# Products of zeros ahead of the first chunk, one weight tile's low part moved from TensorE to VectorE, and a new set of plan numbers, in a kernel that joins linear attention with a gated feed-forward

## The chip, the cores and the metric

The kernel runs on one NeuronCore of a Trainium2 chip. The metric is device time in microseconds (us), as the median of several runs. A profile of one execution goes with it; its time is not one of the runs that make the median. TensorE does the matrix products ("PE" in the rows, "PEld" its weight loads), VectorE is "DVE", ScalarE is "ACT", GpSimd is "POOL", and SyncE ("SP") issues the DMAs.

## The reference

For 4 batches and 8 heads, a state of 48 x 48 decays row by row, takes in the outer product of key and value at each of 768 steps, and is read by the query. The 3072 tokens that come out (384 numbers each) go through an RMS norm and a gated feed-forward with 1536 inner columns.

```python
for t in range(S):
    state = alpha[:, :, t, :, None] * state + np.einsum('bhd,bhe->bhde', k[:, :, t], v[:, :, t])
    y[:, :, t] = np.einsum('bhd,bhde->bhe', q[:, :, t], state)
...
rms = np.sqrt(np.mean(x * x, axis=-1, keepdims=True) + 1e-06)
xn = x / rms * rms_g
g = xn @ w_gate
silu = g * (1.0 / (1.0 + np.exp(-g)))
val = xn @ w_val
return (silu * val @ w_out).astype(np.float32)
```

## The kernel before

**Chunks and groups.** The tokens are cut into 24 chunks of 128 (6 of each batch; chunks 0 to 3 are the first of each batch). Seven groups of 4, 2, 2, 4, 4, 4 and 4 chunks go through the feed-forward one after the other. In group 0 the first five of the twelve inner tiles are done for chunks 0 and 1 and then for chunks 2 and 3, so that the feed-forward can begin when two chunks are there.

**Attention of a chunk.** VectorE runs two scans over the decays (`w`, line 643, with a small reciprocal at 663 between them), multiplies query and key by them (`qp` at 680 in two halves, `kh` at 673). For chunks 0 to 3 everything stays in float32: TensorE turns the keys (line 875), makes the scores (760); VectorE masks them (776); TensorE makes the output `y` (786), the new state (890, in two halves) and the state's part of the output (795); ScalarE squares and sums the output (942), GpSimd takes the root (946, 947), VectorE scales (956, tile `x`), and TensorE turns the result (963, `mm_x`), of which ScalarE takes the high half (971), TensorE subtracts it (977) and ScalarE takes the rest (980). The result is `xT`, the input of the feed-forward. Later chunks work on float16 halves (lines 750, 817, 838, 915).

**Feed-forward.** Each float32 operand is a high and a low float16 half, so that a product takes three passes. For an inner tile f, TensorE multiplies `xT` with the gate and the value weights (line 1131, nine products each); ScalarE makes the silu (1142), VectorE the product with it (1148, called the gate below), ScalarE its high half (491) and VectorE its low half (1161). Line 1201 multiplies with the output weights, VectorE copies out (1212), and SP stores.

**Weights.** A tile of weights (`i0` to `i11` for gate and value, `o0` to `o5` for the output) is loaded as bytes of float64 and made float32 by a ScalarE step (525, the fold) and two VectorE steps (`shift` 530, `join` 533); ScalarE makes the high half (491). The low half is made by VectorE (line 541), but for the tiles named in `LOW_W` by TensorE and ScalarE: two float32 products with a scaled unit matrix (550), from which two float16 products with `minus` (553) take the high half away, and two ScalarE copies (556).

**Order.** Nothing is scheduled by the compiler. `Plan.order` makes one list from a table of costs (`COST`), due times (`DUE`, `GAP`) and shifts (`LATE`, `W_LATE`): at each step the engine that can start first takes, among what can start within 0.12 of that, the operation with the smallest due number. The list is then issued as it stands, and each engine runs its own part strictly in that order. PSUM has three buffers `mm`, three `at` and one `y`.

**Set-up.** Constants are filled by GpSimd and VectorE in the first 6 us. `junk` is a bfloat16 tile of 128 x 384 into which the squares are thrown; its first row serves as `unit`, a row of float32 ones by which TensorE spreads the norm's gains over all partitions (line 614, `mm_rg`).

Of the kernel before, what the change touches and what calls it, by code (L numbers as in the profile page):

```python
# [8 lines left out]
F32 = mybir.dt.float32  # L9
# [41 lines left out]
WIDE = range(10, 24)  # L51
LOW_H = ()
LOW_X = range(4)
LOW_W = ("i0", "i1")

BUFS = dict(
    att=3, w=1, v=3, kh=2, qp=2, k16=2, q16=2, kT=2, v16=4, gd=2, a16=2, ss=2, x32=1, x16=2,
# [1 line left out]
)  # L59

COST = dict(
    scan=1.16, rec=0.13, kh=0.6, qh=0.33, kl=0.6, vl=0.47, ql=0.62, gd=0.12, sd=0.28, sl=0.27, mask=0.59,
    al=0.59, st=0.27, ss=0.12, x=0.46, xl=0.47, shift=0.53, rest=0.88, wl=0.87, ob=0.46,
    dec=0.15, k16=0.62, v16=0.52, q16=0.62, s16=0.26, a16=0.5, sq=0.58, x16=0.53, st0=0.22,
    abs=0.86, odd=0.57, cnt=1.0, wh=0.83, pow=0.8, sc=0.76, sc32=0.9, ys=0.42, ysw=0.38, yv=0.63, yvw=0.57, y32=0.9, add=0.5, take=0.4, u=0.5, po=1.48, xp=0.75, kp=1.3, u32=0.42,
    neg=0.3, wid=0.85, wneg=0.22, wl2=0.37, rgw=0.9, rgt=0.37, x32=0.53, xb=0.37, ys32=0.5, kb=0.45, near=0.34, xneg=0.25,
)
IN_COST = {
    4: (1.95, 0.49, 0.6, 0.63), 3: (1.47, 0.39, 0.47, 0.52), 2: (0.99, 0.28, 0.34, 0.4),
# [4 lines left out]


PACE = [1.0, 1.0, 1.15, 1.18, 1.18, 1.18, 1.18]
GAP = [-5.4, 137.5, 45.8, 79.0, -35.5, -147.4, 300.1]
DUE = [
    -693.9, -491.0, 464.9, -444.6, 227.3, 564.4, 969.3, 214.1, 305.6, 685.2, 893.3, 575.6, 395.1,
    645.7, 528.3, 156.8, 1104.0, 734.3, 817.3, 300.8, 329.7, 361.1, 414.6, 337.4,  # L80
]
LATE = dict(
    a16=97.6, abs=61.6, add=41.2, al=-52.5, cnt=178.7, dec=-135.3, gd=141.7, k16=-182.6, kb=-58.3,
    kh=169.5, kl=74.7, kp=-158.1, ld2=171.2, load=150.3, mask=-114.5, near=72.9, ob=-130.4,
    odd=-190.2, pow=57.4, q16=-118.1, qh=59.8, ql=-30.8, rec=59.8, rest=-78.3, rg=96.3, rgt=-181.3,
    rgw=49.9, s16=7.8, sc=-119.5, sc32=-44.1, scan=250.6, sd=20.3, shift=-35.4, sl=-33.6, sq=106.5,
    st=-123.9, st0=-164.3, take=-51.2, u=-134.6, u32=-60.7, v=169.9, v16=42.6, vl=19.2, wh=190.9,
    wid=-61.7, wl=-196.0, wl2=37.2, wneg=29.8, x=-243.3, x16=-28.4, x32=0.1, xb=-1.8, xl=32.9,
    xneg=81.0, xp=1.9, y32=-23.6, ys=-23.1, ys32=-39.7, ysw=-28.6, yv=-16.5, yvw=-100.7,
)  # L90
LATE_CHECK = 3
W_LATE = [
    -329.2, -491.3, -215.9, -189.0, -124.1, -113.7, -147.5, 9.7, 26.7, -144.3, 45.6, 99.3, 11.9,
    31.8, 264.2, 289.5, 212.6, 338.9,
]
CUTS = [0, 2, 4]
SIDE = [3, 1]


class Plan:  # L100
# [9 lines left out]
    def op(self, engine, cost, fn, deps=(), use=(), due=None, lock=False, kb=0, late=0.0, kind=None, tile=None):  # L110

        o = dict(e=engine, c=cost, fn=fn, d=[d for d in deps if d], u=tuple(use), due=due, lock=lock,
                 kb=kb, late=late, i=len(self.ops), n=[], k=kind, w=tile)
        for d in o["d"]:
            d["n"].append(o)
        for k in o["u"]:
            self.users[k] = self.users.get(k, 0) + 1
        self.ops.append(o)
        return o
# [216 lines left out]
def tile_attn_moe(  # L336
# [12 lines left out]
    nc = tc.nc  # L349
    NC, _, AW = att.shape  # L350
    R = 112
    DM, DFF = w_gate.shape
    P = 128
# [12 lines left out]
    const = ctx.enter_context(tc.tile_pool(name="const", bufs=1))  # L366
# [3 lines left out]
    xp = ctx.enter_context(tc.tile_pool(name="xp", bufs=1))  # L370
# [5 lines left out]
    ps_mm = ctx.enter_context(tc.tile_pool(name="ps_mm", bufs=1, space=PSUM))  # L376
# [18 lines left out]

    plan = Plan()

    def buf(pool, shape, dtype, tag, key):
        name = "_".join(map(str, key)) if isinstance(key, tuple) else key
        return pool.tile(  # L400
            shape, dtype, tag=f"{tag}{plan.slot[tag, key]}", name=f"{tag}_{name}", bufs=1
        )
# [6 lines left out]
    def att_tile(cc):  # L409
        return tile_of(("att", cc), lambda: buf(ain, [P, AW], F32, "att", cc))  # L410
# [4 lines left out]
    def load_v(cc):  # L415
        v = buf(ain, [P, DM], F32, "v", cc)
        tiles["v", cc] = v
        nc.sync.dma_start(v, vtok[src(cc)])
# [5 lines left out]
    rg = const.tile([P, DM], F32, name="rg")  # L424


    seed = const.tile([R, 2, NP, HC + 1], F32, name="seed")
    nc.vector.memset(seed, 0.0)
    nc.vector.memset(seed[:, 0, :, 0:1], S_Q[1] / S_QP)
# [4 lines left out]
    mask = const.tile([P, 1, C], F32, name="mask")  # L434
    near = const.tile([P, 1, HC], F32, name="near")
# [8 lines left out]
    for x, base, step in (  # L444
# [3 lines left out]
            x, x, pattern=[[0, 1], [1, x.shape[-1]]], compare_op=ALU.is_ge, fill=0.0,  # L448
# [9 lines left out]
    for x, value in ((minus, -1.0), (one, 1.0), (same, S_W)):  # L458
        nc.gpsimd.affine_select(
            x, x, pattern=[[1, P]], compare_op=ALU.not_equal, fill=value, base=0,  # L460
# [6 lines left out]
    nc.gpsimd.memset(t_add, T_ADD)  # L467
    mhalf = const.tile([P, 1], F32, name="mhalf")
    nc.gpsimd.memset(mhalf, -0.5)
    junk = const.tile([P, DM], mybir.dt.bfloat16, name="junk")  # L470
    unit = junk.bitcast(F32)[:1, :P]
    nc.gpsimd.memset(unit, 1.0)


    NH = len(GROUPS) * NF + EARLY * (len(CUTS) - 2)
    o_w, o_o = NC, NC + NF
# [11 lines left out]
    dec = const.tile([R, NC, 2, NP], F32, name="dec")  # L488
# [11 lines left out]
    op = plan.op  # L500

    def add(engine, kind, *args, **kw):
        w = kw.get("tile")
        late = LATE.get(kind, 0.0) + (W_LATE[w] if w is not None else 0.0)
        return op(engine, COST[kind], *args, late=late, kind=kind, **kw)
# [3 lines left out]
    def decode(src, dst, name, col):  # L509
# [3 lines left out]
        def load():  # L513
            raw = buf(wst, [P, NW], I64, "raw", name)
            h = 8 * NW // len(src)
            for i, ap_in in enumerate(src):
                k, w = ap_in.shape[1:]
                to = raw.bitcast(U8)[:, i * h : (i + 1) * h].rearrange("p (k b) -> p k b", k=k)
                nc.sync.dma_start(to[:, :, :w], ap_in)
            t["z"], t["t"] = [raw.bitcast(I32).rearrange("p (n two) -> p n two", two=2)[:, :, i] for i in range(2)]  # L520
            t["tf"] = raw.bitcast(F32).rearrange("p (n two) -> p n two", two=2)[:, :, 1]
            t["top"] = raw.bitcast(I8).rearrange("p (n b) -> p n b", b=8)[:, :, 7 - W_FROM]
# [40 lines left out]
        o = add("DVE", "rest", join, [o, f], [raw, wu], lock=True, tile=w)  # L563
        if name in LOW_W:
            ps = [("at", (name, n)) for n in range(2)]
# [37 lines left out]

    states = {}
    state_ops = {}

    def load_rg():
        nc.sync.dma_start(rg[:1], rms_g.unsqueeze(0))
# [638 lines left out]
    def in_steps(g):  # L1247

        if g:
            return [(f, 0, GROUPS[g]) for f in range(NF)]  # L1250
        return [
            (f, c0, c1) for c0, c1 in zip(CUTS, CUTS[1:]) for f in range(EARLY)
        ] + [(f, 0, GROUPS[0]) for f in range(EARLY, NF)]
# [33 lines left out]
    for g, m in enumerate(GROUPS):  # L1287
        now += GAP[g]
        for i in range(m if g else 0):
# [186 lines left out]
```

## Time and profile before

| | |
|---|---|
| median of 3 runs (lowest, highest) | 521.84 us (520.71, 522.1) |
| the profiled execution: its own time, its span from first to last instruction | 521.89 us, 520.2 us |
| busy share of the span: PE, DVE, ACT, POOL | 97%, 74%, 49%, 7% |
| chain that ended last, by engine: PE, DVE, ACT | 86%, 8%, 2% |

Busy time is the time in which an engine had an instruction in work. The chain is followed back from the last instruction: at each step to what released it, or to the instruction before it on its engine. "Idle before" is the time in which the engine had nothing in work ahead of an instruction, with what ended that. A float32 product is two records in the profile. The granted TensorE clock is given as a share of 2.4 GHz.

### The profile page before, as it was taken

The page shows a single profiled execution, that of the slowest core. Times are in us where ns is not written, and L with a number is a line of the kernel's source. Part 1 is how long each engine was busy: PE and PEld are TensorE (multiplying, and loading weights), DVE is VectorE, ACT ScalarE, POOL GpSimd, SP SyncE. Part 2 cuts the span into 40 slices and gives each one's busy share as a digit, 9 for nine tenths or more (in the row PEclk, how much of TensorE's full clock was granted, in tenths as well). Part 3 has the DMA queues.
Part 4 walks back from the last instruction along what each step waited for, and adds up shares of the span by engine and source line. Part 5 has one row for each costly group of instructions (what it writes and reads, how often), then busy time and mean ns, then how long its engine had stood idle before and what let it go on. Part 6 is the DMA issues. An engine that isn't in the chain of part 4 may idle for free.

```text
span 520.2 us, 12190 instructions
## 1 busy us (share of the span) xinstructions
PE 504.3 (97%) x4976; PEld 303.5 (58%) x4976; DVE 385.7 (74%) x731; ACT 254.0 (49%) x671; POOL 37.9 (7%) x86
## 2 busy tenths in 40 slices
PE   4899999999999999999999999999999999999995
PEld 3687854567877886544566544556544456444552
DVE  6879999999999999998799979997454320233303
ACT  2478977634563575644654466656454310233200
POOL 4020000020010011000010001203100000000000
PEclk9999999999999999999999999999999999999999
DMA  8869686635455346462097661208960000000000
GB/s 303 285 217 231 187 244 208 207 101 151 80 114 154 122 70 140 91 147 80 17 252 213 174 217 38 33 15 246 307 208 31 1 15 32 15 1 0 2 32 33
DMA packets 64031, 65.18 MB, mean 125 GB/s; under 512 B 32993, under 2 KB 57570, under 8 KB 63970
## 3 DMA queue, kind: packets, MB, share of 16 engines
q1 hardware_dynamic: 63970, 64.36, 44.2%
q8 instruction: 39, 0.64, 0.5%
q14 instruction: 22, 0.18, 0.1%
HBM read 52.03 MB, written 4.72 MB: 109 GB/s over the span
## 4 chain that ended last, share of the span: by engine, by line
PE 86%; DVE 8%; ACT 2%; issue 1%; DMA 1%; POOL 0%; DVEq 0%; ACTq 0%; POOLq 0%
PE mm L1131 47%; PE mm_po L1201 27%; PE at L750 3%; PE y L838 2%; PE at L915 2%; DVE wu_i L533 1%; PE y L817 1%; DVE h L1148 1%; PE y L786 1%; DVE h L1161 1%; DVE w L643 1%; PE at L875 1%; DVE wg L541 1%; PE at_i L550 1%; PE mm_x L963 1%
## 5 line engine op out<-in xcount | busy, mean ns | idle before, releaser
L1131 PE MATMUL mm<-xT,wg 128*128 128x512 f16 (+1 forms) x1602 | 287.3, 339 | 0.5 <-ACT sl L1142 0.5
L1131 PEld LDWEIGHTS <-wg 128*128 128x128 f16 x1602 | 153.7, 98 | 121.1 <-issue 0.4
L1201 PE MATMUL mm_po<-wo,h 128*128 128x384 f16 x864 | 144.4, 326 | 0.2 <-DVE h L1148 0.2
L1201 PEld LDWEIGHTS <-h 128*128 128x128 f16 x864 | 83.1, 98 | 56.1 <-issue 1.7
L1148 DVE SCALAR_TENSOR_TENSOR h<-mm,sl 128x512 f32<-128x512 f32 (+1 forms) x89 | 51.7, 583 | 48.4 <-PE mm L1131 48.2
L491 ACT ACTIVATE h<-h 128x512 f16<-128x512 f32 (+1 forms) x89 | 48.5, 545 | 75.2 <-DVE h L1148 74.9
L1142 ACT ACTIVATE sl<-mm 128x512 f32<-128x512 f32 (+1 forms) x89 | 45.4, 510 | 50.7 <-PE mm L1131 50.1
L1161 DVE TENSOR_TENSOR h<-h,h 128x512 f16<-128x512 f32 (+1 forms) x89 | 51.5, 584 | 21.3 <-ACT h L491 21.3
L643 DVE TENSOR_TENSOR_SCAN w<-att,seed 112x520 f32<-112x520 f32 x48 | 59.4, 1238 | 2.6 <-DMA att<-att 2.1
L1212 DVE TENSOR_SCALAR ob<-mm_po 128x384 f32<-128x384 f32 x24 | 13.1, 550 | 36.1 <-PE mm_po L1201 36.0
L946 POOL TENSOR_TENSOR ss<-ssq,eps 128x1 f32<-128x1 f32 x24 | 13.0, 542 | 331.6 <-ACT junk L942 331.6
L766 DVE TENSOR_TENSOR at<-at,mask 128x512 f32<-128x512 f32 x40 | 25.9, 690 | 1.8 <-PE at L750 1.5
L865 ACT CAST a<-at 128x512 f16<-128x512 f32 x40 | 22.6, 583 | 8.1 <-DVE at L766 8.0
L868 DVE TENSOR_TENSOR a<-at,a 128x512 f16<-128x512 f32 x40 | 25.9, 683 | 0.0
L680 DVE TENSOR_TENSOR qp<-att,w 112x256 f32<-112x256 f32 x48 | 18.4, 420 | 3.5 <-PE y L795 3.4
L947 POOL TENSOR_TENSOR ss<-ss,mhalf 128x1 f32<-128x1 f32 x24 | 18.8, 783 | 1.9
L491 ACT ACTIVATE k<-kh 112x512 f16<-112x512 f32 x20 | 12.6, 628 | 10.2 <-DVE kh L673 9.4
L491 ACT ACTIVATE q<-qp 112x512 f16<-112x512 f32 x20 | 12.5, 623 | 10.4 <-DVE qp L680 5.6
L750 PEld LDWEIGHTS <-k 48*128 48x128 f16 x480 | 13.4, 94 | 6.3 <-issue 5.1
L666 ACT COPY dec<-w 112x8 f32<-112x8 f32 x24 | 4.9, 203 | 24.9 <-DVE w L643 24.8
L750 PE MATMUL at<-q,k 48*128 48x128 f16 x480 | 16.9, 217 | 0.0
L491 ACT ACTIVATION_READ_ACCUMULATOR h<-h 128x1 f32 x89 | 16.7, 188 | 0.0
(129 smaller groups left out, 449.1 us busy)
## 6 DMA issues: line engine op xcount, KB each, us to landing
att<-att SPq DMA_DIRECT2D x22, 773.0 KB, 4.5
v<-vtok SPq DMA_DIRECT2D x24, 192.0 KB, 3.9
out_dram<-ob SPq DMA_DIRECT2D x24, 192.0 KB, 2.0
raw_c<-w_gate SPq DMA_DIRECT2D x12, 384.0 KB, 4.9
raw_c<-w_val SPq DMA_DIRECT2D x12, 384.0 KB, 5.8
raw_d<-w_out SPq DMA_DIRECT2D x6, 768.0 KB, 4.6
raw_i<-w_gate SPq DMA_DIRECT2D x11, 384.0 KB, 3.9
raw_i<-w_val SPq DMA_DIRECT2D x11, 384.0 KB, 4.5
```

The costliest lines, as they stand in the source:

```text
L491: nc.scalar.activation(dst, src, AF.Copy, scale=scale, accum_out=stat[:rows, col : col + 1])
L643: nc.vector.tensor_tensor_scan(w, x, start.rearrange("r g p c -> r (g p c)"), 0.0, op0=ALU.mult, op1=ALU.add)
L750: nc.tensor.matmul(t["sc"][j][:, p, :], t["k16"][r, x, p, :], t["q16"][r, y, p, :], start=m == 0, stop=m == 2,)
L766: nc.vector.tensor_tensor(t["sc"][j], t["sc"][j], mask.to_broadcast([P, NP, C]), op=ALU.mult)
L865: nc.scalar.copy(a_tile()[:, j, 0], t["sc"][j])
L868: nc.vector.tensor_tensor(a_tile()[:, j, 1], t["sc"][j], a_tile()[:, j, 0], op=ALU.subtract)
L947: nc.gpsimd.tensor_tensor(t["ss"], t["ss"], mhalf, op=ALU.pow)
L1131: nc.tensor.matmul(ps[:, :n], wg[:, f, x, j, kk, :], xT[:, y, kk, cs], start=i == 0, stop=i == 3 * NK - 1,)
L1142: nc.scalar.activation(t["sl"][:, :n], t[0][:, :n], AF.Silu, scale=1.0 / (S_X * S_W))
L1148: nc.vector.scalar_tensor_tensor(t["h"][:, :n], t[1][:, :n], S_H / (S_X * S_W), t["sl"][:, :n], op0=ALU.mult, op1=ALU.mult,)
L1161: nc.vector.tensor_tensor(h16_of(g, f)[:, 1, cs], t["h"][:, :n], h16_of(g, f)[:, 0, cs], op=ALU.subtract)
L1201: nc.tensor.matmul(t[i][:, :DM], h16_of(g, f)[:, x, ts], wo[:, f // 2, y, f % 2, :], start=f == 0 and m == 0, stop=f == NF - 1 and m == 2,)
```

## The change

Fourteen bfloat16 products of 128 x 128 by 128 x 384 (`warm_first`) stand ahead of everything else on TensorE. Their operands are the tile `junk`, which VectorE now fills with zeros at the start (its first row with the float32 ones); GpSimd's fill of that row goes. They write a buffer `mm` that nobody reads. `LOW_W` loses `i1`, so that this tile's low half is made by VectorE's line 541 (now 544). Some costs and all due numbers and shifts of the plan have new values, which changes the order on every engine; the amount of work of every other kind stays. The new file has ten lines more: line 643 is now 653, 875 is 885, 1131 is 1141, and 530, 533, 550 are 533, 536, 553.

```diff
-LOW_W = ("i0", "i1")
+LOW_W = ("i0",)
...
-GAP = [-5.4, 137.5, 45.8, 79.0, -35.5, -147.4, 300.1]
+GAP = [-15.7, 137.0, 36.9, 106.2, -22.7, -134.2, 399.9]
...
+WARM_FIRST = 14
...
+    junk = const.tile([P, DM], mybir.dt.bfloat16, name="junk")
+    unit = junk.bitcast(F32)[:1, :P]
+    nc.vector.memset(junk, 0.0)
+    nc.vector.memset(unit, 1.0)
     seed = const.tile([R, 2, NP, HC + 1], F32, name="seed")
...
-    junk = const.tile([P, DM], mybir.dt.bfloat16, name="junk")
-    unit = junk.bitcast(F32)[:1, :P]
-    nc.gpsimd.memset(unit, 1.0)
...
+    def warm_first():
+        ps = buf(ps_mm, [P, 512], F32, "mm", "warm")
+        for _ in range(WARM_FIRST):
+            nc.tensor.matmul(ps[:, :DM], junk[:, :P], junk, start=True, stop=True)
+
+    op("PE", 4.8, warm_first, [], [("mm", "warm")])
```

TensorE at the program's start, before (`mm_rg` spreads the gains, `kh_0` is the key of chunk 0, `at` and `y` are PSUM tiles):

```order
L614 MATMUL mm_rg_170<-rg_90,junk_135 128x384
L875 MATMUL at_0_4_183<-one_115,kh_0_181 128x112 x4
L760 MATMUL at_0_0_194<-qp_0_177,kh_0_181 64x64 x2
L760 MATMUL at_0_1_195<-qp_0_177,kh_0_181 64x64 x2
...
```

and now:

```order
L613 LDWEIGHTS junk_91
L613 MATMUL mm_warm_150<-junk_91 128x384
...
L613 MATMUL mm_warm_150<-junk_91 128x384
L624 MATMUL mm_rg_188<-rg_90,junk_91 128x384
L885 MATMUL at_0_4_199<-one_118,kh_0_197 128x112 x4
L770 MATMUL at_0_0_208<-qp_0_193,kh_0_197 64x64 x2
L770 MATMUL at_0_1_209<-qp_0_193,kh_0_197 64x64 x2
...
```

Fourteen pairs of load and product now stand ahead of the first useful product; they wait for VectorE's fill of the row of ones, its third instruction.

VectorE between the second chunk's key and the third chunk's scans, before (`wu_i1`, `wu_i0` are weight tiles in work, `a16_1` the masked scores of chunk 1, `x32_0` the scaled output of chunk 0):

```order
L530 TENSOR_SCALAR wu_i1_302<-raw_i1_162 128x768
L680 TENSOR_TENSOR qp_2_307<-att_2_158,w_2_249 112x4x64 x2
L776 TENSOR_TENSOR a16_1_310<-at_1_0_284,near_98 128x256
L776 TENSOR_TENSOR a16_1_310<-at_1_1_285,near_98 128x256
L533 SCALAR_TENSOR_TENSOR wu_i1_302<-raw_i1_162,wu_i1_302 128x768
L956 SCALAR_TENSOR_TENSOR x32_0_318<-y_0_220,ss_0_312,rg_90 128x384
L673 TENSOR_TENSOR kh_2_326<-att_2_158,w_2_249 112x2x4x64
L530 TENSOR_SCALAR wu_i0_334<-raw_i0_174 128x768
L533 SCALAR_TENSOR_TENSOR wu_i0_334<-raw_i0_174,wu_i0_334 128x768
L643 SCALAR_TENSOR_TENSOR w_3_373<-att_3_190,seed_91 112x520
```

and now:

```order
L533 TENSOR_SCALAR wu_i1_300<-raw_i1_178 128x768
L690 TENSOR_TENSOR qp_2_320<-att_2_171,w_2_265 112x4x64
L536 SCALAR_TENSOR_TENSOR wu_i1_300<-raw_i1_178,wu_i1_300 128x768
L786 TENSOR_TENSOR a16_1_327<-at_1_0_302,near_101 128x256
L786 TENSOR_TENSOR a16_1_327<-at_1_1_303,near_101 128x256
L690 TENSOR_TENSOR qp_2_320<-att_2_171,w_2_265 112x4x64
L544 SCALAR_TENSOR_TENSOR wg_146<-wu_i1_300,wg_146 128x768
L966 SCALAR_TENSOR_TENSOR x32_0_339<-y_0_234,ss_0_329,rg_90 128x384
L533 TENSOR_SCALAR wu_i0_342<-raw_i0_190 128x768
L683 TENSOR_TENSOR kh_2_348<-att_2_171,w_2_265 112x2x4x64
L536 SCALAR_TENSOR_TENSOR wu_i0_342<-raw_i0_190,wu_i0_342 128x768
L653 SCALAR_TENSOR_TENSOR w_3_372<-att_3_206,seed_94 112x520
```

The low half of `i1` (line 544) now stands on VectorE ahead of the scaling of chunk 0, and the join of `i1` ahead of the mask of chunk 1.

TensorE right behind the scores of chunk 1, before, with the float32 products of both weight tiles:

```order
L550 MATMUL at_i1_0_320<-wu_i1_302,same_114 128x384
L963 MATMUL mm_x_0_328<-one_115,x32_0_318 128x128 x3
L550 MATMUL at_i1_1_337<-wu_i1_302,same_114 128x384
L786 MATMUL y_1_342<-v_1_166,a16_1_310 64x48 x16
...
L553 MATMUL at_i1_1_337<-wg_145,minus_112 128x384
L795 MATMUL y_1_342<-sd1_379,qp_1_218 64x48 x8
L550 MATMUL at_i0_0_394<-wu_i0_334,same_114 128x384
L550 MATMUL at_i0_1_400<-wu_i0_334,same_114 128x384
```

and now:

```order
L973 MATMUL mm_x_0_344<-one_118,x32_0_339 128x128 x3
L796 MATMUL y_1_350<-v_1_186,a16_1_327 64x48 x16
L987 LDWEIGHTS minus_115
L987 MATMUL mm_x_0_344<-xT_0_370,minus_115 128x384
...
L553 MATMUL at_i0_0_389<-wu_i0_342,same_117 128x384
L805 MATMUL y_1_350<-sd1_394,qp_1_251 64x48 x8
L553 MATMUL at_i0_1_408<-wu_i0_342,same_117 128x384
```

The two products of `i1` are gone, so that behind the scores of chunk 1 TensorE's next instruction is the turn of chunk 0, which waits for VectorE's `x32_0`.

On SP, the load of chunk 2's `att` now stands ahead of chunk 0's `v`, of the second part of chunk 1's `att` and of the weights `i1`.

## Rows read from the trace of the kernel before

**Rows 1.** The page's first part: busy us, share of the span and instructions of each engine.

```profile
PE 504.3 (97%) x4976; PEld 303.5 (58%) x4976; DVE 385.7 (74%) x731; ACT 254.0 (49%) x671; POOL 37.9 (7%) x86
```

**Rows 2.** Busy time by stretch: its us, then PE, PEld, DVE, ACT, POOL busy us (instructions), the granted clock, the DMA engines' share and GB/s.

```profile
0.00:20.00 20.00, 12.19 (x162) 10.14 (x162) 14.07 (x26) 5.73 (x13) 6.10 (x35) 1.00 0.87 313
40.00:60.00 20.00, 18.74 (x328) 15.96 (x327) 19.07 (x38) 17.84 (x51) 1.48 (x4) 1.00 0.85 212
60.00:120.00 60.00, 59.77 (x491) 34.14 (x489) 58.98 (x103) 39.71 (x94) 2.97 (x2) 1.00 0.65 192
120.00:240.00 120.00, 120.00 (x1656) 84.73 (x1655) 116.80 (x246) 64.64 (x199) 6.85 (x14) 1.00 0.48 113
240.00:360.00 120.00, 120.00 (x1240) 65.42 (x1237) 108.87 (x206) 68.83 (x182) 13.51 (x18) 1.00 0.47 128
```

**Rows 3.** TensorE in one piece (timeline: start us, us, what), two pieces of the chain late in the program (start us, us, what), and the only wait of TensorE from 62 us on (us in total, times, longest).

```profile
57.04 37.24 PE L1131 MATMUL mm<-xT,wg 128*128 128x256 f16 x216
```

```profile
373.18 46.62 PE mm L1131 x216
419.80 23.40 PE mm_po L1201 x144
```

```profile
PE mm_po L1201 <- DVE h L1148: 0.2, 1, 0.2
```

**Rows 4.** The chain that ended last, at the start of the program: start us, us, what.

```profile
8.10 2.05 PE at L875 x8
...
11.80 1.96 PE y L786 x30
...
18.19 1.05 PE at L760 x30
```

**Rows 5.** TensorE's timeline from 18 to 38 us: start us, us, line, operation, tiles, shapes, records, and in brackets the idle time before and what ended it.

```profile
21.03 1.62 PE L550 MATMUL at_i<-wu_i,same 128*128 128x384 f32 x2 [1.80 <-DVE wu_i L533]
...
25.14 1.63 PE L786 MATMUL y<-v,a 64*64 64x48 f32 x32
26.70 0.34 PE L977 MATMUL mm_x<-xT,minus 128*128 128x384 f16 x1
26.97 0.66 PE L890 MATMUL at<-v,kT 64*64 64x48 f32 x16
...
28.07 0.67 PE L795 MATMUL y<-sd,qp 48*64 48x48 f32 x16
28.67 1.56 PE L550 MATMUL at_i<-wu_i,same 128*128 128x384 f32 x4
30.06 0.49 PE L553 MATMUL at_i<-wg,minus 128*128 128x384 f16 x2
...
31.07 1.15 PE L875 MATMUL at<-one,kh 112*128 112x112 f32 x8
32.15 0.69 PE L760 MATMUL at<-qp,kh 48*64 48x64 f32 x32
32.77 0.94 PE L963 MATMUL mm_x<-one,x 128*128 128x128 f32 x6
33.54 1.04 PE L875 MATMUL at<-one,kh 112*128 112x112 f32 x8
34.52 1.08 PE L786 MATMUL y<-v,a 64*64 64x48 f32 x30
...
37.64 0.61 PE L1131 MATMUL mm<-xT,wg 128*128 128x256 f16 x4
```

**Rows 6.** What VectorE waited for up to 34 us: us in total, times, longest.

```profile
DVE qp L680 <- PE y L795: 3.4, 2, 2.3
...
DVE a L776 <- PE at L760: 1.2, 2, 0.7
...
DVE x L956 <- POOL ss L947: 0.4, 1, 0.4
DVE wu_i L533 <- ACT raw_i L525: 0.4, 1, 0.4
```

**Rows 7.** VectorE's timeline, with columns as in rows 5.

```profile
12.66 0.69 DVE L673 TENSOR_TENSOR kh<-att,w 112x512 f32<-112x512 f32 x1
...
20.80 0.61 DVE L956 SCALAR_TENSOR_TENSOR x<-y,ss,rg 128x384 f32<-128x384 f32 x1
...
28.79 0.76 DVE L680 TENSOR_TENSOR qp<-att,w 112x256 f32<-112x256 f32 x2 [2.31 <-PE y L795]
```

**Rows 8.** Groups of VectorE instructions of one shape over the whole span: busy us, mean ns of one, idle before.

```profile
L643 DVE TENSOR_TENSOR_SCAN w<-att,seed 112x520 f32<-112x520 f32 x48 | 59.4, 1238 | 2.6 <-DMA att<-att 2.1
...
L541 DVE SCALAR_TENSOR_TENSOR wg<-wu_i,wg 128x768 f16<-128x768 f32 x10 | 9.5, 945 | 0.0
```

**Rows 9.** Two stretches of the tail, with columns as in rows 2.

```profile
514.00:515.00 1.00, 0.61 (x4) 0.16 (x2) 0.36 (x2) 0.00 (x0) 0.00 (x0) 1.00 0.00 0
...
518.00:519.00 1.00, 0.00 (x0) 0.00 (x0) 0.00 (x0) 0.00 (x0) 0.00 (x0) 0.50 0.02 8
```

**Rows 10.** The program's start in the timeline of all engines, with columns as in rows 5.

```profile
0.98 0.49 DVE L428 MEMSET seed<- 112x520 f32 x1 [0.98 <-PEq L1465]
...
3.73 1.24 DVE L643 TENSOR_TENSOR_SCAN w<-att,seed 112x520 f32<-112x520 f32 x1 [2.11 <-DMA att<-att]
...
6.16 1.65 PE L614 MATMUL mm_rg<-rg,junk 1*128 1x384 f32 x2 [6.16 <-POOL junk L472]
```

More of the change, by code (lines that the diff above doesn't have):

```diff
@@ L61 @@
 COST = dict(
-    scan=1.16, rec=0.13, kh=0.6, qh=0.33, kl=0.6, vl=0.47, ql=0.62, gd=0.12, sd=0.28, sl=0.27, mask=0.59,
+    scan=1.16, rec=0.18, kh=0.6, qh=0.33, kl=0.6, vl=0.47, ql=0.62, gd=0.12, sd=0.28, sl=0.27, mask=0.59,
     al=0.59, st=0.27, ss=0.12, x=0.46, xl=0.47, shift=0.53, rest=0.88, wl=0.87, ob=0.46,
-    dec=0.15, k16=0.62, v16=0.52, q16=0.62, s16=0.26, a16=0.5, sq=0.58, x16=0.53, st0=0.22,
-    abs=0.86, odd=0.57, cnt=1.0, wh=0.83, pow=0.8, sc=0.76, sc32=0.9, ys=0.42, ysw=0.38, yv=0.63, yvw=0.57, y32=0.9, add=0.5, take=0.4, u=0.5, po=1.48, xp=0.75, kp=1.3, u32=0.42,
-    neg=0.3, wid=0.85, wneg=0.22, wl2=0.37, rgw=0.9, rgt=0.37, x32=0.53, xb=0.37, ys32=0.5, kb=0.45, near=0.34, xneg=0.25,
+    dec=0.2, k16=0.62, v16=0.52, q16=0.62, s16=0.26, a16=0.5, sq=0.58, x16=0.53, st0=0.28,
+    abs=0.86, odd=0.57, cnt=1.0, wh=0.83, pow=0.8, sc=0.76, sc32=0.8, ys=0.42, ysw=0.38, yv=0.63, yvw=0.57, y32=1.12, add=0.5, take=0.4, u=0.5, po=1.48, xp=0.9, kp=1.15, u32=0.66,
+    neg=0.3, wid=0.85, wneg=0.33, wl2=0.37, rgw=0.7, rgt=0.37, x32=0.53, xb=0.37, ys32=0.66, kb=0.5, near=0.34, xneg=0.28,
 )
@@ L76 @@
 PACE = [1.0, 1.0, 1.15, 1.18, 1.18, 1.18, 1.18]
-GAP = [-5.4, 137.5, 45.8, 79.0, -35.5, -147.4, 300.1]
+GAP = [-15.7, 137.0, 36.9, 106.2, -22.7, -134.2, 399.9]
 DUE = [
-    -693.9, -491.0, 464.9, -444.6, 227.3, 564.4, 969.3, 214.1, 305.6, 685.2, 893.3, 575.6, 395.1,
-    645.7, 528.3, 156.8, 1104.0, 734.3, 817.3, 300.8, 329.7, 361.1, 414.6, 337.4,
+    -719.9, -428.4, 411.3, -551.6, 184.4, 443.0, 1038.8, 186.9, 211.3, 740.5, 1018.7, 654.7, 756.4,
+    831.8, 770.0, 432.6, 1179.9, 1019.1, 1109.0, 512.2, 336.7, 338.7, 475.6, 483.2,
 ]
 LATE = dict(
[L83 to L89, printed above, removed]
+    a16=95.7, abs=95.5, add=-3.0, al=-37.8, cnt=239.3, dec=-143.8, gd=128.7, k16=-225.5, kb=-100.3,
+    kh=211.5, kl=37.3, kp=-148.6, ld2=204.9, load=96.2, mask=-127.2, near=132.3, ob=-144.7,
+    odd=-153.0, pow=73.9, q16=-96.0, qh=38.4, ql=-11.4, rec=52.2, rest=-69.8, rg=8.7, rgt=-201.8,
+    rgw=-6.4, s16=44.3, sc=-125.2, sc32=-36.5, scan=303.9, sd=70.9, shift=-71.0, sl=-52.1, sq=109.6,
+    st=-82.7, st0=-193.5, take=-59.8, u=-107.2, u32=-53.5, v=186.2, v16=124.3, vl=-14.9, wh=160.7,
+    wid=-93.7, wl=-301.4, wl2=15.7, wneg=80.9, x=-230.4, x16=-36.5, x32=-16.4, xb=-7.0, xl=-43.5,
+    xneg=126.0, xp=27.6, y32=-52.5, ys=-23.6, ys32=-78.8, ysw=-43.9, yv=-74.0, yvw=-116.3,
 )
@@ L92 @@
 W_LATE = [
-    -329.2, -491.3, -215.9, -189.0, -124.1, -113.7, -147.5, 9.7, 26.7, -144.3, 45.6, 99.3, 11.9,
-    31.8, 264.2, 289.5, 212.6, 338.9,
+    -285.5, -492.0, -249.7, -250.4, -99.8, -149.6, -106.2, -73.2, 53.8, -132.7, 151.4, 126.2, 126.8,
+    172.8, 286.5, 195.7, 182.1, 333.3,
 ]
+WARM_FIRST = 14
 CUTS = [0, 2, 4]
```

## The prediction

> **What bounds the kernel now.** I read the page's busy shares first: TensorE 97%, VectorE 74% [rows 1]. A share over the whole span hides stages, so the second view is busy time by stretch [rows 2]: in the first 20 us TensorE is busy for 12.19 us and VectorE for 14.07; from 40 to 240 us VectorE has hardly a gap (19.07 of 20, 58.98 of 60, 116.80 of 120), and only behind 240 does it get room (108.87 of 120). TensorE's timeline shows from where it is full: at 57.04 us one piece of 216 feed-forward products begins, and from 62 us on its only wait is 0.2 us [rows 3]. Late in the program, where nothing disturbs it, 216 wide products take 46.62 us (216 ns each) and 144 output products 23.40 us (162.5 ns each) [rows 3]: that is a stream without holes. So behind 57 us the time is TensorE's work, and the time of the end moves by what is earlier at 57 us and by what TensorE no longer has to do, as long as VectorE, which is full up to 240 us, keeps up.
>
> Ahead of 57 us I read the chain and the timeline. From 8.10 to about 27 us the chain is nearly all TensorE [rows 4], and the same instructions take longer there than later: eight records of line 875 take 2.05 us at 8.10 and 1.15 and 1.04 us at 31.07 and 33.54; line 786 takes 1.96 at 11.80, 1.63 at 25.14 and 1.08 at 34.52; two records of line 550 take 1.62 at 21.03, and four take 1.56 at 28.67 [rows 4, 5]. That is a factor near 2, TensorE's two clock levels, 1.2 and 2.4 GHz, with the rise between 25.14 and 26.97. The granted clock in the profile's rows reads 1.00 from the start [rows 2]: it shows no change there, the durations do. Only the fall at the end is recorded (0.50 from 518 us, after the last product in the microsecond from 514) [rows 9]. VectorE pays for the low clock in waits for TensorE: 3.4 us ahead of `qp`, 1.2 us ahead of the masks, and 0.4 + 0.4 for others, 5.4 us in all [rows 6].
>
> **The change, part by part.**
>
> *The zeros.* No row shows such a product. The nearest, 384 columns at the high clock, takes 162.5 ns [rows 3]; at half the clock that is 325. Fourteen take 2.3 to 4.6 us. They can start when VectorE has filled `junk`, `seed` and the row of ones: 0.98 + 0.49 for `seed` [rows 10], and by that row at most 0.49 for `junk`, so near 2.0 us, and they end by 6.6. VectorE's first scan waits for its DMA until 3.73, so the fills cost nothing. Behind them `mm_rg` takes 1.65 us at most [rows 10] and ends by 8.2; line 875 of chunk 0 waits for `kh` until 8.10. Cost 0 to 0.1 us; I take 0.
>
> *The clock.* If it is up when chunk 0 arrives, the pieces of [rows 4] shrink to the later durations of [rows 5]. The waits of VectorE go: the scores of chunk 0 come 0.9 us sooner (line 875 alone), which ends the first mask's wait; `qp` of chunk 2 and the mask of chunk 1 wait no more. Up to `x32_0`, which began at 20.80 [rows 7], that is 1.1 (the first of the two `qp` waits, 3.4 less the 2.31 at 28.79 [rows 6, 7]) + 1.2 = 2.3 us. The moved low half puts 0.9 us back (mean 945 ns [rows 8]). So `x32_0` begins near 19.4 and ends near 20.0 us.
>
> From there I count TensorE's queue in the new order to the first feed-forward product, by the later rows of [rows 5], from 26.70 on: turn 0.94, `y` of chunk 1 1.08, line 977 0.34, line 890 0.66, the two products of `i0` 1.56, line 795 0.67, line 553 0.49, line 890 0.66, then chunk 3 and 2: 1.15, 0.69, 0.94, 1.04, 1.08, 0.66, 0.34, 0.69, 0.67. Sum 13.7, so the first one starts at 33.7 instead of 37.64: 3.9 us earlier. In this sum lies what the change takes from TensorE: two float32 products and two subtractions of `i1`, 1.56 + 0.49 = 2.05 us at the high clock. ScalarE loses two copies; it is not the bound.
>
> *VectorE.* It gains 5.4 us of waits; I leave 0.4 of them, since the waits for GpSimd and ScalarE may stay: 5.0. It gets 0.9 of low half, and by the order one more scan (1.24 [rows 8]) stands ahead of the last copy-out of group 0; all other kinds are as many as before up to there. That leaves 2.9 us by which VectorE is earlier where it is full.
>
> *The loads.* Ahead of chunk 0's `v` now stand 2.0 MB; at the 313 GB/s of the first 20 us [rows 2] they land by 8 us, and line 786, which wants `v`, began at 11.80 [rows 4]. Cost 0.
>
> *The rest of the plan.* Behind 57 us TensorE has 0.2 us of waits to win [rows 3], so a new order can only lose there, or nothing. Bounds: 0 to 1 us of loss; I take 0.
>
> *Sum.* TensorE's count gives 3.9 us, VectorE's 2.9. VectorE bounds where it has no gap, to 240 us, but the feed-forward takes its results with three PSUM buffers between, which lets it lag by part of a step. I take 3.4, the middle: 521.89 - 3.4 = 518.5 for an execution like the profiled one, which lies 0.05 above the median of the runs: 518.4.
>
> **A rule that speaks against it.** Between 11.80 and 19.23 us TensorE works in the chain without a break [rows 4], and the clock stays low; the small float32 products did not lift it, so they may not hold it either. In the new order TensorE has nothing to do from the end of chunk 1's scores (near 16.1: the key of chunk 1, 13.35 before [rows 7], comes 0.5 sooner without the first mask's wait, then 1.15 + 0.67 + 0.66 + 0.69) to `x32_0` at 20.0, a hole of nearly 4 us; in the tail the fall is on record some 3 us after the last product [rows 9]. The Trainium skill (TensorE: Matmul & The Clock Gate, section "HAM oscillation") says that idle gaps between bursts of products send the clock back to half, each burst then starting slow. The tail agrees. By that rule the change's gain would end at the hole; this is the second case below.
>
> **The rivals.**
>
> 1. *The clock falls in the hole.* Then the queue from 20.0 runs at half speed until full-size products lift it, as those from 21.03 on did some 5 us later [rows 5]. In 5.3 us it does work of 2.7: the first feed-forward product comes near 36.3 instead of 33.7, and 1.3 us of the gain remain by TensorE. VectorE keeps about 1 us of its second `qp` wait: 2.9 - 1 = 1.9. Middle 1.6: 520.2 us.
>
> 2. *The change doesn't do what it says: zeros don't lift the clock.* Then the waits stay but for what the order changes (the join of `i1` now lies in the mask's wait): VectorE wins back about 2.4 us of 5.4 and pays 0.9 + 1.24, so 0.3; TensorE's removed products, 3.2 at the low clock (twice 1.62 of line 550 [rows 5]), are eaten by a later `x32_0` and by a clock that rises later. About 521.6 us, no change. Against it: nothing in the trace says what zeros do.
>
> 3. *Slower: the clock rises later than before.* What stands right ahead of the rise in before are full-size float32 products, among them both of `i1` (21.03 and on, [rows 5]), and these go. If the zeros don't hold and TensorE then stays at half speed until 32 us or later, 5 us more at half speed cost 2.5 us at a place where TensorE has no gaps, against 0.3 to 0.9 us gained: 523.5 us. The turning point is a rise near 28 us.
>
> 4. *More than counted:* VectorE follows TensorE's 3.9 and some loss between 40 and 57 us goes too (20 - 18.74 us [rows 2]): 5 us, 516.8.
>
> **How the numbers follow.** The forecast holds 0.57, with its own range of 517.4 to 519.4; rival 1 holds 0.19, rival 2 0.09, rival 3 0.10, rival 4 0.05. A change of less than 0.3% (1.57 us) can't be told from none, so "faster" is below 520.3. The forecast and rival 4 lie there (0.62), with half of rival 1 (0.09): 0.71. "Same" takes the other half and most of rival 2, 0.18; "slower" is rival 3 and a bit of rival 2, 0.11. The range reaches over rivals 1 and 2 and leaves out most of rivals 3 and 4: 516.9 to 521.7.
>
> **What would show it.** Line 885 (old 875) of chunk 0 near 1.15 us for eight records, and the float32 products of lines 796 and 553 at the durations of [rows 5], mean that the clock was up and held; doubled durations behind 20 us mean rival 1, from the start on rival 2. VectorE's waits up to 34 us should fall from 5.4 to under 1 us. The first feed-forward product should start near 34 us, and the full stream near 53.5 instead of 57.04. Behind that, TensorE's waits should stay under 1 us; if VectorE's gate becomes a wait of several us between 60 and 240 us, the extra 2.1 us on VectorE were what decided, and the forecast is too good.

## The result, and the profile after

The changed kernel takes **525.26 us** (median of 13 executions, 520.7 to 531.1) against 521.79 us for the kernel before in the same runs (13, 520.71 to 522.53): ratio **1.0064, 95% interval 1.0039 to 1.0089**. The prediction was 518.4 us with a range of 516.9 to 521.7: the direction is wrong, and the median lies outside. The spread grew too, from 1.8 us to 10.4 us. The profiled execution took 523.55 us (span 521.7), so it is one of the quicker ones; what a longer one looks like is read from a second profile, below.

The views of before have their counterparts here; lines of the program lie 3 to 10 higher (550 is now 553, 875 is 885, 1131 is 1141). First, the page's busy shares, as in [rows 1]:

```profile
PE 508.2 (97%) x4984; PEld 305.8 (59%) x4984; DVE 387.9 (74%) x734; ACT 254.3 (49%) x669; POOL 30.9 (6%) x85
```

Then busy time by stretch, with the columns of [rows 2]:

```profile
0.00:20.00 20.00, 16.75 (x176) 12.09 (x176) 14.83 (x27) 6.13 (x14) 6.30 (x34) 1.00 0.88 310
20.00:40.00 20.00, 18.00 (x259) 14.12 (x260) 16.31 (x30) 11.42 (x30) 2.05 (x5) 1.00 0.72 216
40.00:60.00 20.00, 19.09 (x270) 16.36 (x268) 19.90 (x38) 17.66 (x52) 1.75 (x3) 1.00 0.84 228
60.00:120.00 60.00, 58.27 (x547) 33.80 (x546) 58.27 (x103) 40.50 (x95) 1.81 (x4) 1.00 0.64 187
120.00:240.00 120.00, 120.00 (x1581) 84.86 (x1579) 112.50 (x235) 62.85 (x195) 5.47 (x14) 1.00 0.43 108
```

In the first 20 us TensorE is busy for 4.56 us more than before; 4.66 us of that are the zeros. Behind 20 us TensorE is busy for less in two stretches: 60 to 120 us (58.27, where 59.77 stood) and 20 to 40 us (18.00, where 18.96 stood in this row of before):

```profile
20.00:40.00 20.00, 18.96 (x272) 14.73 (x273) 16.75 (x30) 12.90 (x32) 2.99 (x4) 1.00 0.67 213
```

VectorE has more room from 120 to 240 us (112.50 of 120, 116.80 before), so it didn't become the bound there.

TensorE's timeline, with the columns of [rows 5]:

```profile
1.87 4.66 PE L613 MATMUL mm_warm<-junk 128*128 128x384 bf16 x14 [1.87 <-DVE seed L436]
6.46 1.64 PE L624 MATMUL mm_rg<-rg,junk 1*128 1x384 f32 x2
8.29 2.02 PE L885 MATMUL at<-one,kh 112*128 112x112 f32 x8 [0.19 <-DVE kh L683]
...
22.00 1.65 PE L973 MATMUL mm_x<-one,x 128*128 128x128 f32 x6 [2.62 <-DVE x L966]
23.58 1.95 PE L796 MATMUL y<-v,a 64*64 64x48 f32 x32
...
26.91 1.65 PE L553 MATMUL at_i<-wu_i,same 128*128 128x384 f32 x2
28.49 1.09 PE L805 MATMUL y<-sd,qp 48*64 48x48 f32 x16
29.51 1.65 PE L553 MATMUL at_i<-wu_i,same 128*128 128x384 f32 x2
...
31.52 0.66 PE L900 MATMUL at<-v,kT 64*64 64x48 f32 x16
32.11 1.15 PE L885 MATMUL at<-one,kh 112*128 112x112 f32 x8
...
38.43 4.76 PE L1141 MATMUL mm<-xT,wg 128*128 128x256 f16 x42
```

Fourteen zeros in 4.66 us are 333 ns each: the low clock. Line 885 takes 2.02 us, as before the change; in this execution the zeros did not lift the clock at all. And the durations halve only near 31 us (line 900 at 31.52, line 885 at 32.11), while in before they did so near 26 [rows 5]. The first feed-forward product starts at 38.43 instead of 37.64.

VectorE's waits up to 34 us, as in [rows 6], and the waits of TensorE over the whole span:

```profile
DVE qp L690 <- PE y L805: 3.5, 2, 2.4
...
DVE a L786 <- PE at L770: 1.1, 2, 0.6
...
DVE x L966 <- POOL ss L957: 0.4, 1, 0.4
```

```profile
PE mm_x L973 <- DVE x L966: 3.0, 2, 2.6
...
PE mm_po L1211 <- issue: 1.7, 1, 1.7
```

Of 5.4 us of VectorE's waits 0.4 went. The wait of 1.7 us ahead of line 1211 stands at 103.4 us; the profile names no releaser for it.

**Where the time of this execution went.** Idle time of TensorE by the stretches above and [rows 2]: 0 to 20 us 7.81 before, 3.25 after (the zeros fill it); 20 to 40 us 1.04 and 2.00; 40 to 60 us 1.26 and 0.91; 60 to 120 us 0.23 and 1.73: 2.45 less in all, while it is busy for 3.9 us more, so the span grows by 1.5 us. Without the zeros TensorE's busy time is 503.5 instead of 504.3: two products and two subtractions went, but what stands between 26 and 31 us ran at half speed and gave most of that back. The 1.5 us is about as large as the gap at 103.4 us; the expected gain ahead of it never came.

### The profile page after: what moved, and what is told of

Same layout as the page of the kernel before. It is cut to its first block, busy times and chain, and to the rows that moved or that the text cites. A ratio compares the mean times of both kernels' runs of the same rounds, so it can differ in the third digit from the quotient of the medians.

```text
span 521.7 us, 12197 instructions
## 1 busy us (share of the span) xinstructions
PE 508.2 (97%) x4984; PEld 305.8 (59%) x4984; DVE 387.9 (74%) x734; ACT 254.3 (49%) x669; POOL 30.9 (6%) x85
## 4 chain that ended last, share of the span: by engine, by line
PE 92%; DVE 3%; issue 1%; ACT 1%; DVEq 0%
PE mm L1141 53%; PE mm_po L1211 27%; PE at L760 3%; PE y L848 2%; PE at L925 1%; PE y L827 1%; PE at L885 1%; PE y L796 1%; DVE wu_i L536 1%; PE at_i L553 1%; PE at L900 0%; DVE w L653 0%; ACT raw_i L528 0%; DVE wg L544 0%; DVE a L786 0%
## 5 line engine op out<-in xcount | busy, mean ns | idle before, releaser
L956 POOL TENSOR_TENSOR ss<-ssq,eps 128x1 f32<-128x1 f32 x24 | 10.1, 422 | 356.2 <-ACT junk L952 356.2
L683 DVE TENSOR_TENSOR kh<-att,w 112x512 f32<-112x512 f32 x24 | 16.4, 684 | 0.0
L957 POOL TENSOR_TENSOR ss<-ss,mhalf 128x1 f32<-128x1 f32 x24 | 14.7, 614 | 1.9
```

## The experiments

The theory: what decides is when the clock comes back up for good. In before the two products of `i1` bring that about near 26 us; the change takes them out, and the zeros' own lift does not last. Its rivals: the new plan itself costs the time, or the zeros do. "The hole" is TensorE's wait ahead of the turn of chunk 0. Times are medians of three batches, each with the kernel before beside it: 521.53 us beside the changed kernel again, no zeros, before + zeros and zeros in the hole; 521.25 us beside start and 20 in the hole and the other two runs of the kernel before; 521.61 us beside the rest.

| run | median us (lowest to highest, n) | ratio to before, 95% | first feed-forward product, span of the profile |
|---|---|---|---|
| changed kernel again | 526.37 (522.74 to 529.12, 12) | 1.0062 to 1.0110 | 41.73, 526.4 |
| no zeros | 522.61 (519.83 to 528.50, 12) | 1.0010 to 1.0052 | 35.81, 518.1 |
| six zeros | 523.38 (520.61 to 530.09, 12) | 1.0007 to 1.0053 | 38.27, 521.9 |
| before + zeros | 520.57 (520.24 to 521.88, 12) | 0.9976 to 0.9995 | 36.14, 518.8 |
| before, `i1` by VectorE | 526.42 (523.69 to 528.45, 6) | 1.0059 to 1.0113 | 39.17, 524.7 |
| `i1` back | 521.75 (519.40 to 523.28, 12) | 0.9990 to 1.0017 | 34.77, 518.9 |
| zeros in the hole | 519.70 (519.37 to 523.71, 12) | 0.9955 to 0.9983 | 34.41, 517.9 |
| start and hole | 518.53 (517.96 to 519.02, 5) | 0.9927 to 0.9954 | 34.55, 517.2 |
| start and 20 in the hole | 519.47 (518.90 to 520.11, 5) | 0.9952 to 0.9978 | 36.13, 518.1 |
| clock held | **516.34** (516.10 to 518.76, 5) | 0.9884 to 0.9914 | 34.60, 517.0 |
| before, clock held | 517.42 (517.34 to 517.54, 5) | 0.9913 to 0.9939 | 32.74, 515.7 |

**The changed kernel again.** No edit; a second profile and twelve times.

> The changed kernel once more. Theory A (the zeros lift the clock in most executions, it falls back soon behind them, and it comes up for good only when full-size products follow, which without i1's two is later and varies): times scatter again over 8 us or more (520 to 530), the mean granted clock lies between 0.960 and 0.985 in most executions, and a profile with such a clock shows a stretch at 0.50 that begins before 20 us and ends between 25 and 50. Theory B (the clock does the same each time, the new order on VectorE or later in the plan costs the time): a stretch at 0.50, if any, is the same length in each execution, and the profile shows TensorE waiting between 60 and 240 us for several us.

The median confirms the loss. The scatter is 6.4 us, less than expected, and all twelve mean clocks lie between 0.962 and 0.979. This profile (of an execution of 528.10 us) shows the other course. TensorE's timeline, columns as above:

```profile
1.87 4.18 PE L613 MATMUL mm_warm<-junk 128*128 128x384 bf16 x14 [1.87 <-DVE seed L436]
5.98 0.91 PE L624 MATMUL mm_rg<-rg,junk 1*128 1x384 f32 x2
8.13 1.38 PE L885 MATMUL at<-one,kh 112*128 112x112 f32 x8 [1.24 <-DVE kh L683]
...
28.77 1.65 PE L553 MATMUL at_i<-wu_i,same 128*128 128x384 f32 x2
...
36.48 1.89 PE L885 MATMUL at<-one,kh 112*128 112x112 f32 x8
...
41.17 0.63 PE L805 MATMUL y<-sd,qp 48*64 48x48 f32 x16
```

Windows of half a microsecond of the same kernel; the granted clock is the third number from the end:

```profile
8.00:8.50 0.50, 0.37 (x3) 0.41 (x4) 0.43 (x1) 0.00 (x0) 0.00 (x0) 1.00 1.04 387
8.50:9.00 0.50, 0.50 (x6) 0.50 (x6) 0.50 (x1) 0.00 (x0) 0.00 (x0) 0.83 1.09 445
9.00:9.50 0.50, 0.50 (x7) 0.30 (x8) 0.47 (x2) 0.15 (x1) 0.00 (x0) 0.50 0.94 367
...
39.00:39.50 0.50, 0.50 (x14) 0.50 (x14) 0.22 (x2) 0.28 (x2) 0.00 (x0) 0.50 0.91 299
39.50:40.00 0.50, 0.50 (x22) 0.50 (x22) 0.50 (x2) 0.00 (x0) 0.00 (x0) 0.95 1.10 385
```

Here the zeros did lift the clock while they ran (4.18 us for fourteen, then line 624 in 0.91 instead of 1.64). It fell again near 8.8 us, with line 885 running behind a wait of 1.24 us, and came back only near 39.6. The products of `i0` ran at the low clock on the way (28.77). The first feed-forward product is 4.09 us later than before.

**The zeros taken out, or cut to six.**

```diff
     def warm_first():
-        ps = buf(ps_mm, [P, 512], F32, "mm", "warm")
-        for _ in range(WARM_FIRST):
-            nc.tensor.matmul(ps[:, :DM], junk[:, :P], junk, start=True, stop=True)
+        return
```

> The changed kernel without the fourteen products of zeros, in the same order otherwise. A: no fall is recorded (mean clock 0.996 to 0.998 in each execution), the clock comes up near 31 us as in the changed kernel's profile, times near 523.5 with a scatter of 2 us or less, so faster than the changed kernel by 1 to 2 us in the median. B: the zeros are neutral, the median stays at 525 with the same scatter.

Six zeros: `WARM_FIRST = 6`.

> The changed kernel with six products of zeros at the start instead of fourteen (2 us of work instead of 4.7). A without C: as with none, 522.6, scatter from 520 to 528. C: too few to lift the clock, so as with none too; if they lift it all the same in many executions, the median goes to 525 or 526 as with fourteen.

Without zeros the same order is still slower than before and still scatters, 519.83 to 528.50 us: the scatter does not come from the zeros. Neither expectation for this run came true: the median lies below 523.5 us, and the scatter is 8.7 us and not 2. The execution that was profiled is the lowest of them, and its TensorE timeline shows an early return:

```profile
25.26 0.49 PE L985 MATMUL mm_x<-xT,minus 128*128 128x384 f16 x1
25.68 0.66 PE L898 MATMUL at<-v,kT 64*64 64x48 f32 x16
26.27 0.91 PE L553 MATMUL at_i<-wu_i,same 128*128 128x384 f32 x2
...
35.81 5.09 PE L1139 MATMUL mm<-xT,wg 128*128 128x256 f16 x45
```

With the clock up near 25.7, about as in before, this order is 2.1 us shorter (span 518.1 against 520.2). So the new order is not at fault as such; what it lost is a return at the same time in each execution. Six zeros, at the low clock throughout (2.10 us), do as none. The fourteen make it worse than none: in one batch 526.37 against 522.61, with intervals of the ratio that don't meet (that of the first thirteen executions, 1.0039 to 1.0089, does meet the one of no zeros).

**Each half of the change on the kernel before.** The zeros ahead of everything, with VectorE's fill of `junk` in place of GpSimd's (not printed here); nothing else changed:

```diff
     with tc.manual_schedule():
-        for o in plan.order():
+        ordered = plan.order()
+        ps = ps_mm.tile([P, 512], F32, tag="mm2", name="mm_warm", bufs=1)
+        for _ in range(14):
+            nc.tensor.matmul(ps[:, :DM], junk[:, :P], junk, start=True, stop=True)
+        for o in ordered:
             o["fn"]()
```

> The kernel before with the fourteen products of zeros ahead, nothing else changed. A: the clock is lifted and falls in most executions (mean clock below 0.99), and it comes up again near 26 us, since i1's products stand where they stood: 519 to 522, scatter 3 us at most, no worse than before. B: the same or faster than before by what the clock gives, 517 to 522. If the fall itself costs the time, whatever the plan is, this one scatters up to 530 too.

And the low part of `i1` by VectorE, without zeros and with the old plan's numbers:

```diff
-LOW_W = ("i0", "i1")
+LOW_W = ("i0",)
```

> The kernel before with i1's low part made by VectorE, no zeros, the plan's numbers as before. A: without i1's full-size products the clock comes up late and at varying times: times from 520 to 530, median 522 to 525, profile with line 550's two products at the low clock. If the plan's numbers are what makes it scatter: 521 to 522.5 with the scatter of before.

With the zeros alone the clock rises, falls at 10.2 us in the 1.33 us gap behind chunk 0's scores, and comes back at 23.8, under the second of `i1`'s two products: 1.0 us less in the medians (521.53 to 520.57), with a scatter of 1.6 us, as was expected. TensorE's timeline:

```profile
7.98 1.12 PE L876 MATMUL at<-one,kh 112*128 112x112 f32 x8 [0.47 <-DVE kh L674]
...
11.05 1.95 PE L787 MATMUL y<-v,a 64*64 64x48 f32 x30 [1.33 <-DVE a L777]
...
22.97 1.24 PE L551 MATMUL at_i<-wu_i,same 128*128 128x384 f32 x2
24.15 1.14 PE L787 MATMUL y<-v,a 64*64 64x48 f32 x32
```

With the low part alone the time goes up by about 5 us, more than expected, and the timeline shows why the first microsecond and a half of it:

```profile
28.71 2.93 PE L550 MATMUL at_i<-wu_i,same 128*128 128x384 f32 x4
31.43 0.85 PE L553 MATMUL at_i<-wg,minus 128*128 128x384 f16 x2
...
33.09 1.15 PE L875 MATMUL at<-one,kh 112*128 112x112 f32 x8
...
39.17 6.07 PE L1131 MATMUL mm<-xT,wg 128*128 128x256 f16 x54
```

The products of `i0` ran at the low clock (2.93 us for four records, 1.56 in [rows 5]) and the return came behind them. The other 3 us of this profile's 4.5 are waits behind that, 1.4 and 0.6 us for a feed-forward weight among them. That suggests that the old plan's numbers don't fit the moved work, so that a new plan could mend this part of the loss; no run separates it.

**`i1` back on TensorE in the changed kernel,** zeros and the plan's numbers kept: `LOW_W = ("i0", "i1")`.

> The changed kernel, zeros and new plan numbers kept, but with i1's low part made by TensorE again. A: i1's two products stand ahead of chunk 0's turn again and lift the clock between 22 and 28 us, so 519 to 522, scatter 2 us or less, and faster than the changed kernel by 4 us or more. B (the new order itself is at fault): 524 or more.

The time is that of before again, and the scatter falls from 10 us to 4 (2 was expected). The two float32 products of `i1` (four records, 2.90 us) now run from 18.75 us, in the hole, and the clock is up behind them (line 796 at 22.57: 1.14 us). But TensorE has the 2.05 us of `i1` to do again, which would be why nothing is gained: zeros, which cost it nothing there, take 519.70 us in the next experiment.

**Zeros in the place of `i1`'s products.** Eight zeros ahead of the turn of chunk 0, into the same PSUM tile, from a tile of their own; first without the zeros at the start, then with them, then with twenty.

```diff
         def x_across():
             t["xp"] = buf(ps_mm, [P, NK, C], F32, "mm", key("x"))
+            for _ in range(8 if cc == 0 else 0):
+                nc.tensor.matmul(
+                    t["xp"].rearrange("p k c -> p (k c)"), zero[:, :P], zero, start=True, stop=True,
+                    skip_group_check=True,
+                )
```

> The changed kernel without zeros at the start, but with eight products of zeros of the same size in TensorE's wait ahead of the turn of chunk 0 (19.4 to 22.0 us in the profile), where the old order had i1's first product. A: they do what i1's products did: the clock comes up between 24 and 29 us instead of 31, times near 521, scatter 2 us or less. B: nothing changes against the kernel without any zeros.

> The changed kernel with its fourteen products of zeros at the start and eight more in the wait ahead of chunk 0's turn. Theory A (what decides is when the clock comes up for good): the early lift falls back again, the eight products bring the clock up near 22 us in every execution, so 519 to 520.5 with a scatter of 2 us or less, as with the eight alone (519.7). Theory C (the lift and fall themselves do harm, for instance because the clock then comes back later): 522 or more, with scatter.

> The changed kernel with 14 products of zeros at the start and 20 ahead of chunk 0's turn, none between. A: the clock falls in between and comes back near 22 us, so 518 to 519.5, 2 us behind the kernel with fills in every wait. If the fills between do nothing: 516.3.

TensorE's timeline of the first of these:

```profile
19.04 2.74 PE L973 MATMUL mm_x<-zero 128*128 128x384 bf16 x8
21.73 1.29 PE L978 MATMUL mm_x<-one,x 128*128 128x128 f32 x6
22.95 1.14 PE L796 MATMUL y<-v,a 64*64 64x48 f32 x32
```

The zeros ran at the low clock (2.74 us for eight) in time that TensorE was waiting anyway, the turn behind them saw it rise, and line 796 behind that takes 1.14 us where the changed kernel took 1.95. That alone turns the +0.3% of no zeros into -0.3%; with the zeros at the start as well it is -0.6%. (One of the twelve executions with eight zeros took 523.71 us, so the scatter is 4.3 us and not 2.) So the zeros at the start do no harm once something brings the clock back. That they give the second 0.3% is not shown: in the profile with them they don't lift the clock (4.66 us), the first feed-forward product starts no earlier (34.55 against 34.41), and the span is 0.7 us shorter where a wait of 1.7 us at line 1211 is missing, which only the other profile has. Twenty in the hole are not better than eight: in the profile they take 5.59 us and outlast the wait, and the turn of chunk 0 starts at 23.91 us instead of 21.98.

**The clock held.** Zeros in every early wait of the changed kernel, the 14 at the start kept: 8 ahead of the key turn of chunk 0, 8 ahead of its outputs, 4 and 6 ahead of chunk 1's key turn and scores, 20 ahead of chunk 0's last turn.

```diff
+    def fill(to, n):
+        for _ in range(n):
+            nc.tensor.matmul(to, zero[:, :P], zero[:, : to.shape[-1]], start=True, stop=True, skip_group_check=True)
...
+            if cc in (0, 1):
+                fill(t["kp"].rearrange("p n r -> p (n r)")[:, :DM], (8, 4)[cc])
...
+            if cc == 0:
+                fill(t["xp"].rearrange("p k c -> p (k c)"), 20)
```

> The changed kernel with products of zeros in each of TensorE's early waits: 14 at the start, then 8, 8, 4, 6 and 20 ahead of the key's turn, the output, the second chunk's turn, its scores and chunk 0's scaled turn. A: the clock comes up at the start and holds, no stretch at 0.50 after 10 us, VectorE's waits up to 34 us fall under 2 us, the first feed-forward product starts near 33 us: 517 to 519. If it falls all the same between the fills: 519 to 521, since the twenty bring it back near 22 us. If the fills delay useful products: above 521.

The same zeros in the kernel before, 12 of them ahead of the first product of `i1`:

> The kernel before with 14 products of zeros at the start and fills in its early waits (8, 8, 4 and 6 where the kernel with fills has them, and 12 ahead of i1's first product). Theory A: the clock holds here too, so most of the 5 us comes without the new plan: 517 to 519, and what is left to 516.3 is the new plan's and i1's moved low part. If the gain hangs on the new plan: 520 or more.

Both beat both kernels. In the second one's profile the clock comes up within the first zeros and never falls ahead of the feed-forward; from its TensorE timeline:

```profile
1.53 3.88 PE L1406 MATMUL mm_warm<-junk 128*128 128x384 bf16 x14 [1.53 <-DVE junk L432]
...
8.07 1.11 PE L890 MATMUL at<-one,kh 112*128 112x112 f32 x8 [0.41 <-DVE kh L682]
...
13.55 1.04 PE L890 MATMUL at<-one,kh 112*128 112x112 f32 x8
...
18.93 0.81 PE L555 MATMUL at_i<-wu_i,same 128*128 128x384 f32 x2
...
32.74 0.50 PE L1146 MATMUL mm<-xT,wg 128*128 128x256 f16 x3
```

The held clock is worth 3.8 us on the kernel before (521.25 to 517.42). The plan and the moved low part add 1.1 us by the medians (517.42 to 516.34); these are two batches, and the intervals of their ratios touch, so the size is not settled. The profile of the held changed kernel is of its slowest execution, 518.76 us. There the zeros ran at the low clock, the key turn of chunk 0 began at 10.23 us (8.29 in the changed kernel), and it took 1.40 us, so the clock came up under it. The other four executions lie between 516.10 and 516.42, below what was expected; that the clock held from the start in them is not shown by a profile.

## Why the prediction was wrong

**The zeros at the start: right.** They took 4.66 us, just over the upper bound given (4.6), in time that was idle; line 885 starts 0.19 us later than before.

**"If it is up when chunk 0 arrives", and holds: the step that failed.** In 3 of the 13 timed executions no fall is on record (mean granted clock above 0.99), and the one with a profile shows that the zeros never lifted it. In the others a fall is recorded. The four profiles that show one, of this kernel and of three others with zeros at the start (before + zeros, `i1` back, start and 20 in the hole), have it between 8.5 and 10.2 us, long before the hole (16.1 to 20.0 us by the prediction), where the first rival had it. So a lift by zeros ahead of 6.5 us did not last through the work of chunk 0. The rule cited against the change (the Trainium skill, "TensorE: Matmul & The Clock Gate", section "HAM oscillation") says that gaps between bursts send the clock back to half. The traces agree in part: the fall at 10.2 us of before + zeros lies in a gap of 1.33 us, but in the other three TensorE was at work when it came, 0.5 to 1.3 us behind the end of a gap of 1.1 to 1.3 us. I gave a fall 0.19 and only one place to act.

**"In this sum lies what the change takes from TensorE", 2.05 us as a gain: right by itself, wrong in what it left out.** The products are gone from the queue, but they were also what stood ahead of the rise. The runs show that this is the cause: taking them out of before costs about 5 us, some 1.5 of it ahead of the feed-forward; putting them back in the changed kernel gives 521.75 us; eight zeros in their place give 518.53 us with the zeros at the start, and without those 519.70 where no zeros took 522.61. The third rival named this mechanism and priced it at 523.5 us for a rise at 32 us. The profile with a rise near 31 took 523.55, but a wait of 1.7 us at line 1211 is in that, which the rival didn't have, so the agreement is partly luck. Its chance of 0.10 was too low, and the return scatters up to 39.6 us, which I had not foreseen. What it cost can be read from the mean clocks. Two of the 13 executions, 528.11 us at a mean granted clock of 0.966 and 520.70 at 0.982 (spans 526.3 and 518.9), spent about 2 x 0.034 x 526.3 = 36 and 2 x 0.018 x 518.9 = 19 us at half speed behind their fall, the end of the program included: 7.4 us for 17 us, 0.43 us for each microsecond. A straight line through all ten executions with a fall gives 0.39, through the twelve of the run "changed kernel again" 0.33. The rival was reckoned with a half.

**VectorE.** The waits were to fall from 5.4 to under 1 us; 5.0 are left, as the clock stayed low. The low half moved to it costs 0.96 us at 20.46, as reckoned (0.945 in [rows 8]). `x32_0` was to begin near 19.4 us; it begins at 21.34, 0.54 later than before [rows 7]. From 60 us on no wait of TensorE for VectorE is left in the profile, so VectorE did keep up.

**The first feed-forward product** was to start at 33.7 us: `x32_0` ready at 20.0, and 13.7 us of queue behind it. With eight zeros in the hole the turn of chunk 0 starts at 21.73 and 21.98 us, and the first product 12.7 and 12.6 us later, at 34.41 and 34.55. So the queue was reckoned about 1 us too long and its start nearly 2 us too early, and the two partly cancel. The other sign, a full stream from 53.5 us on, came nearly true in the first profile (54.37) though nothing was gained, and the second has it at 57.07, as before, and is 6.2 us longer: where the stream begins hangs on the order too.

**"I take 3.4, the middle": too little for the clock that it supposes.** 518.53 us with zeros at the start and in the hole lies near the 518.4 that were forecast, but that is luck: its profile does not show the course that was forecast, as line 885 (there 887) still takes 2.02 us. With zeros in every wait it is 516.34 us, 5.3 below the kernel before beside it (521.61), more than TensorE's 3.9 and VectorE's 2.9, and near the fourth rival's 516.8.

**"The rest of the plan", bounds 0 to 1 us of loss: too narrow.** The gap at 103.4 us costs 1.7 us in the changed kernel's first profile, and between 0.4 and 2.0 in four other runs of this plan (none, zeros in the hole, six zeros, again), but it is missing in the runs with zeros at start and hole or held. No releaser is shown, and what it waits for stays open.

**Still open:** why fourteen zeros that lift the clock for a while make its return later than none. The second profile shows that course; the medians (526.37 against 522.61) and the mean clocks say that a late return is the usual one. No run separates its cause.

## What to carry to other kernels

Ask of every product that a change removes from an early stage whether the clock's rise stands right behind it; if so, its removal is no gain until something else stands there. Where TensorE waits early in a program, full-size products of zeros that fit into each of these waits can hold the clock, which was worth 3.8 us on the kernel before; a burst at the start alone was worth 1.0 us there, and twenty zeros in a wait that was too short for them delayed what stood behind. Where the time hangs on a clock that may or may not rise, one profile shows one course: read the spread of the times first, and take a second profile.

## What the runs showed that was not expected

- Products of zeros lift the clock, but not in each execution: fourteen took 4.66 us in one profile of the changed kernel, 4.18 in the other, 3.88 in the held kernel before (at the low clock throughout it is 4.66).
- Small float32 products without a gap did not bring the clock back soon: from 26 to 39.5 us in the second profile TensorE works without a gap, full-size products of `i0` among them, and stays at the low level.
- The granted clock reads 1.00 until the first change that is recorded, also where durations show half speed: in the run with no zeros an execution of 525.45 us has a mean of 0.998, the one of 519.83 us has 0.999. A late first rise is seen in durations alone.
